# Fixed ScalarE steps of three and of two score tiles in turn, in an attention and FFN kernel

## The chip, the cores and the metric

One core of one Trainium2 chip. The metric is device time in microseconds (us) of one execution. The kernel before takes 705.39 us (median of 3 runs, 705.05 to 706.08). A run counts as slow when it is over 1.5% above the fastest of the same kernel; slow runs are left out of all ratios. Within 2% of before is called the same. The *granted clock* is the share of its full clock that the profile shows for PE. The engines are PE (TensorE), ACT (ScalarE), DVE (VectorE), POOL (GpSimd) and SP (SyncE, which here issues DMAs).

## The reference

A layer norm feeds two branches whose results are added to the input: attention with 32 query heads on one key and value head, and an FFN with a squared ReLU.

```python
xn = _layernorm(x)                      # S = 2048, D = 640
q  = (xn @ wq)  -> 32 heads of 20       # k = xn @ wk, v = xn @ wv: one head of 20
p  = softmax(q k^T * 20 ** -0.5)        # 32 x 2048 x 2048
a  = (p v, heads joined) @ wo
h  = relu(xn @ w1 + b1) ** 2            # F = 1536
return x + a + (h @ w2 + b2)
```

The 32 x 2048 x 2048 scores are made in 32 blocks of 4 heads and 512 queries. Each has 16 key tiles, so there are 32 x 16 x 4 = 2048 score tiles of 128 keys by 512 queries. A tile fills one PSUM bank.

## The kernel before

The program is made by a list scheduler in Python: it keeps a model of each engine's time and appends whichever operation can start first. The order is fixed when the kernel is built. What matters for this change:

- A *step* is one ScalarE instruction that takes the exponential of two or three neighbouring banks. One *score pass* of PE fills them, with up to four tiles side by side in four row groups.
- VectorE takes a part of the tiles away from ScalarE (L1083: one tile from its bank into an integer approximation, then three passes for each set of four tiles on VectorE or GpSimd). Such a tile usually rides along in the row groups that a step's pass leaves free. A pass for a VectorE tile alone is called an *own pass* here; it carries one tile.
- The projections and FFN units, one at a time, also need a bank until VectorE evicts it, and P times V (the exponentials times the values) collects in a bank of its own over a whole block of 4 heads and 512 queries.

```python
NB = 7                      # banks 0 to 6 are shared out freely
PVB = 7                     # bank of P times V
STATIC = False
R3 = 2                      # a step of three only if 3 + R3 banks are free
KEEP = 1                    # one free bank is always left
...
def make_step():
    j = len(steps)
    if par("STATIC"):
        banks = list(SIDES[j % 2])
        if any(bank_state(bk) is None for bk in banks):
            return None
        return build_step(j, banks, 0.0)
    ...
    if len(ok) >= 3 + par("R3"):
        ...                                       # three neighbouring banks
...
def pool_banks():           # banks for VectorE tiles and for units
    if par("STATIC"):
        return [bk for bk in POOLED if bk not in HELD and bank_state(bk) is not None]
    fb = [bk for bk in POOLED if bank_state(bk) is not None]
    return fb if len(fb) > par("KEEP") else []
...
# an own pass: only if the next step's pass is more than DGAP = 0.5 us off,
# and ranked (DQP = 3) behind P times V (1) and the units (0.9, 2)
if rd is not None and (nq is None or nq > max(free["PE"], rd) + par("DGAP")):
    consider("PE", par("DQP"), r[0], ("dqk",) + r[1:])
...
# PE would be idle for long: filler matmuls with zero weights are put in
f_ = Op("fill", "PE", 0.2205, fill_parts())
```

The RULES table sets such knobs by stages of 10 us of ScalarE's time. It had been searched for this kernel.

The softmax here doesn't subtract the row's maximum and nothing guards it: scores larger than these inputs give would overflow.

Of the kernel before, what the change touches and what calls it, by code (L numbers as in the profile page):

```python
# [16 lines left out]
NBLK = QC * G  # L17
# [8 lines left out]
EPS = 1e-5  # L26
# [9 lines left out]
def _pl(z):  # L36
# [9 lines left out]
NB = 7  # L46
PVB = 7
SHARED = (4, 5, 6)
STATIC = False
SIDES = ((0, 1), (2, 3))  # L50
POOLED = tuple(range(NB))
HELD = sum(SIDES, ())
EVP = 0.8
# [27 lines left out]
RULES = {3: {'PVA': 2.1, 'PVD': 2.1, 'R3': 1, 'PP': 0.9},  # L81
         4: {'PVA': 2.1, 'PVD': 2.1, 'R3': 1, 'PP': 0.9, 'WARM': 0.78},
         5: {'D1P': 1, 'MPRIO': 0.5, 'PBIAS': 2.5},
         6: {'D1P': 1, 'MPRIO': 0.5, 'PBIAS': 2.5, 'ND': 1, 'QKP': 0},
         7: {'DQP': 2.05, 'URG': 2, 'PVD': 2.1, 'BEHIND': -0.3},
         8: {'WARM': 0.85, 'DQP': 0.95},
         10: {'ND': 1, 'NOPEN': 3},
         11: {'ND': 1, 'NOPEN': 3},
         12: {'EPS': 0.12},
         13: {'EPS': 0.06, 'EVP': 0.3},  # L90
         15: {'PBIAS': 0},
         17: {'EPS': 0.06},
         18: {'EPS': 0.12},
         19: {'WARM': 0.78, 'PBIAS': 2.5, 'IDLE': 0.3},
         21: {'PBIAS': 0, 'KEEP': 0},
         23: {'EPS': 0.12},
         25: {'R3': 1, 'EVP': 0.3},
         26: {'R3': 1, 'EVP': 0.3, 'IDLE': 0.3, 'PVD': 2.1},
         28: {'EPS': 0.12, 'URG': 3},
         29: {'EPS': 0.12, 'URG': 3, 'KEEP': 3, 'EVP': 1.1, 'ND': 3},  # L100
         31: {'PBIAS': 1, 'D1P': 1, 'PVD': 1.05},
         32: {'PBIAS': 1, 'D1P': 1, 'PVD': 1.05, 'DGAP': 0.8, 'DQP': 0.95, 'SQP': 2, 'R3': 1},
         36: {'PP': 0.9, 'BEHIND': -0.1, 'EVP': 0.3, 'PBIAS': 1.5},
         37: {'URG': 3, 'JIT': 1.0, 'PVD': 1},
         38: {'SQP': 0.7, 'URG': 3},
         39: {'PP': 2.5},
         40: {'PBIAS': 1},
         41: {'PBIAS': 1, 'DGAP': 1.5, 'SQP': 0.7},
         42: {'PBIAS': 1, 'DGAP': 1.5, 'SQP': 2, 'NOPEN': 3, 'ND': 2, 'PVD': 1},
         43: {'PBIAS': 1, 'DGAP': 1.5, 'SQP': 2, 'NOPEN': 3, 'ND': 2, 'PVD': 1, 'R3': 9},  # L110
         44: {'WARM': 0.78, 'KEEP': 3, 'DLAST': 7.5},
         45: {'DGAP': 0.8, 'KEEP': 1, 'D1P': 3},
         48: {'PBIAS': 1},
         49: {'PBIAS': 1, 'R3': 1},
         50: {'PBIAS': 1, 'R3': 1},
         53: {'DLAST': 3.5},
         54: {'DLAST': 3.5, 'EPS': 0, 'EVP': 0.3},
         55: {'DLAST': 3.5, 'EPS': 0, 'EVP': 0.3, 'ND': 1},
         56: {'EVP': 2, 'MPRIO': 1.0},
         57: {'R3': 1, 'ND': 1},  # L120
         58: {'BEHIND': -0.1, 'EPS': 0, 'PP': 4, 'R3': 1},
         59: {'BEHIND': -0.1, 'EPS': 0, 'PP': 4, 'R3': 1, 'DRATE': 0.95, 'DLAST': 10, 'PVA': 2.1},
         60: {'EVP': 1.1},
         61: {'EVP': 1.1, 'SQP': 0.7},
         62: {'EVP': 1.1, 'SQP': 0.7, 'KEEP': 3, 'R3': 1, 'NOPEN': 2, 'D1P': 3},
         64: {'PP': 0.9, 'DRATE': 0.8},
         65: {'R3': 1},
         66: {'R3': 1},
         67: {'EPS': 0.12, 'PVA': 1.05},
         68: {'R3': 0},  # L130
         69: {'R3': 0, 'JIT': 1.1}}
HOOK = None
PRIO = {'NM15': 2.12, 'NM10': 2.88, 'PW2': 0.96}
NBEF = {'AG4': 10.21, 'NM7': 11.5, 'Qe0_1': 10.11, 'PW12': 25.33}
XACT = (1, 3)
QEACT = (0, 1, 2, 3)
# [7 lines left out]
FFN0 = 0.3  # L144
# [4 lines left out]
ACTST = (2, 5, 6)  # L149
POOLXN = (2, 7, 9, 10, 11, 13, 14, 15)  # L150
# [9 lines left out]
                EPS=0.03, JIT=JIT, R3=R3, STATIC=STATIC, PVA=1, PVD=1, D1P=1, PP=4, SQP=2, DQP=3, QKP=0, ND=2, WARM=WARM, KEEP=KEEP)  # L160
# [64 lines left out]
def bass_parallel_sum__grouped_kv_mqa__dense_activation_squared_relu__prompt_kernel(nc, A_x, A_wq, A_wk, A_wv, A_wo, B_x, B_w1, B_b1, B_w2, B_b2, out):  # L225
    es = ExitStack()
    with es:  # L227
# [138 lines left out]
        def mm(out_, l, r, start, stop, tp):  # L366
            return lambda e: e.matmul(out_, l, r, start=start, stop=stop, tile_position=tp)  # L367
# [138 lines left out]
        def fill_parts():  # L506
            return [mm(ps[32 * jj:32 * jj + 32, PVB, :], zeros32[:, :], kT[:, 0:512], False, False, (0, 32 * jj)) for jj in range(4)]

        def warm_parts():
            return [lambda e: e.matmul(ps[:, PVB, :], ones_bf[:, :], hT_tmp[:, 0, :], start=True, stop=True)]  # L510

# [337 lines left out]
# [6 lines that stand above are left out]
                    return None  # L855
                return build_step(j, banks, 0.0)
            t0 = max(free["PE"], horizon() - par("JIT"))
            st_of = {bk: bank_state(bk) for bk in range(NB)}
            ok = [bk for bk in range(NB) if st_of[bk] is not None and st_of[bk] <= t0 + 0.02]
            banks = None  # L860
            if len(ok) >= 3 + par("R3"):
                ap = [(a, a + d, a + 2 * d) for d in (1,) for a in range(NB - 2 * d) if {a, a + d, a + 2 * d} <= set(ok)]
                if ap:
                    banks = list(ap[0])
            if banks is None:
                can = sorted((max(st_of[bk], st_of[bk + 1], t0), bk) for bk in range(NB - 1) if st_of[bk] is not None and st_of[bk + 1] is not None)
                if not can:
                    return None
                banks = [can[0][1], can[0][1] + 1]
            return build_step(j, banks, t0)  # L870
# [50 lines left out]

        def make_pv(b, kt):
            first, last = b not in pv_begun, pv_count[b] == KT - 1
            parts, deps = [], []
            for h in range(HPG):
                o, sl = tile_act[(b, kt, h)]
                deps.append(o)
                parts.append(mm(ps[32 * h:32 * h + 32, PVB, :], vx[:, kt, :], PT[:, sl, :], first, last, (0, 32 * h)))
            deps.append(v_op[kt // 4])
            if first and b > 0:  # L930
                deps.append(tn_op[b - 1])
            return Op(f"PV{b}_{kt}", "PE", 0.222, parts, deps)

        def make_dpv(s, term):
            b, kt, n = s["b"], s["kt"], s["n"]
            first, last = b not in pv_begun, pv_count[b] == KT - 1 and len(s["terms"]) == 1
            src, wgt = tbuf(s["buf"][term]), (vx if term == 0 else vxs[:, term - 1, :, :])
            deps = list(s["made"][term])
            parts = []
            for h in range(HPG):  # L940
                i = s["order"].index(h)
                parts.append(mm(ps[32 * h:32 * h + 32, PVB, :], wgt[:, kt, :], src[:, i * 512:(i + 1) * 512], first, last, (0, 32 * h)))
            deps.append(v_op[kt // 4])
            if term:
                deps.append(vs_op[kt // 4][term - 1])
            if first and b > 0:
                deps.append(tn_op[b - 1])
            return Op(f"DPV{b}_{kt}_{term}", "PE", 0.2205, parts, deps)
# [14 lines left out]
        def emit_norm(b, lastpv):  # L963
            marg = DMARG if b < NBLK - 3 else DMEND
            qc, g = divmod(b, G)
            a = b % NOR
            if b >= NBLK - 2:
                Tn, T2 = OR[:, a, :], QCr[:, 0, :]
                tn = op(f"TN{b}", "DVE", 0.63, lambda e: e.transpose(out=Tn, in_=ps[:, PVB, :]), [lastpv] + or_users[a], prio=0)
# [8 lines left out]
            tn = op(f"TN{b}", "DVE", 0.60, lambda e: e.tensor_copy(out=OR[:, a, :], in_=ps[:, PVB, :]), [lastpv] + or_users[a], prio=0)  # L978
# [62 lines left out]
        def pool_banks():  # L1041

            if par("STATIC"):
                return [bk for bk in POOLED if bk not in HELD and bank_state(bk) is not None]
            fb = [bk for bk in POOLED if bank_state(bk) is not None]
            return fb if len(fb) > par("KEEP") else []
# [5 lines left out]
        def make_dqk(heads):  # L1052
            opn = [s for s in sets[-NL:] if s["left"]]
            fb = pool_banks()
            if not fb or (len(fb) == 1 and behind()):
                return None
# [60 lines left out]
        def tail_bank():  # L1117
            done = not peek_tiles(1)[0]
            bs = [bk for bk in range(NB) if (bk not in HELD or done) and bank_state(bk) is not None]
            if tn_op.get(NBLK - 1) is not None and tn_op[NBLK - 1].fin is not None and not bank_busy[PVB]:  # L1120
                bank_rel[PVB] = bank_rel[PVB] or tn_op[NBLK - 1]
                bs.append(PVB)
            return min(bs, key=lambda bk: (bank_state(bk), bk)) if bs else None
# [68 lines left out]
        while True:  # L1192
# [37 lines left out]
            if b < NBLK and (b == 0 or b - 1 in tn_op):  # L1230
# [76 lines left out]
            elif kind == "qk":  # L1307
                take_step(ap[1])
                heads = [t[2] for t in ap[1]["tiles"]]
                while len(heads) < HPG:  # L1310
# [13 lines left out]
            elif kind == "pv":  # L1324
                pv_begun.add(ap[1])
                pv_of[(ap[1], pv_ready[ap[1]].pop(ap[2])[1])] = o
                finish_pv(ap[1], o)
            elif kind == "dpv":
                pv_begun.add(ap[1])
# [129 lines left out]
```

## Time and profile before

| | before |
|---|---|
| time, us | 705.39 |
| busy: PE, ACT, DVE, POOL | 99%, 98%, 92%, 61% |
| ScalarE steps of two, of three | 665, 50 |
| tiles on ScalarE, on VectorE | 1480, 568 |
| filler groups of four matmuls | 3 |

The chain of work that ended last lies on ScalarE for 95%. From the waits of before (engine, line, what it waited for: us in total, times, longest):

```profile
DVE tmore L1083 <- PE ps L367: 28.2, 83, 1.3
```

VectorE, before one of its score tiles, was idle for 28 us in total until PE had filled the bank.

### The profile page before, as it was taken

To read this page: it belongs to the slowest core of one execution; us is meant where nothing else is said; L and a number is where in the kernel's file an instruction comes from. 1 tells how busy PE (TensorE), PEld (TensorE's weight loads), DVE (VectorE), ACT (ScalarE), POOL (GpSimd) and SP (SyncE) were. 2 spreads that over 40 slices of the span, in tenths; PEclk is the share of its full clock that TensorE was granted. 3 is DMA by queue.
4 is the path that set the end of the run, shared out by engine and by line. 5 is a ranking of instruction groups with operands and counts; after the bars stand their busy time and mean duration, and the time that the engine had idled before them with its cause. 6 is when DMAs were issued, how large, how long until landed. Compare 5 with 4: busy or idle time off the path is not lost.

```text
span 703.6 us, 22608 instructions
## 1 busy us (share of the span) xinstructions
PE 695.0 (99%) x9780; PEld 216.0 (31%) x9781; DVE 645.9 (92%) x1125; ACT 687.5 (98%) x739; POOL 427.3 (61%) x268
## 2 busy tenths in 40 slices
PE   8999999999999999999999999999999999999997
PEld 4422223233322223332322222323333222233333
DVE  7789999999999998989998998899899999999894
ACT  6899999999999999999999999999999999999995
POOL 4767556567566764666568765766665675644253
PEclk9999999999999999999999999999999999999999
DMA  6325422233337701211101001111112100031201
GB/s 201 98 70 153 115 78 58 81 97 80 84 85 160 162 20 25 55 40 37 52 18 40 23 22 28 29 47 26 46 42 51 36 22 23 20 106 51 55 26 39
DMA packets 42016, 44.00 MB, mean 63 GB/s; under 512 B 15540, under 2 KB 32772, under 8 KB 41788
## 3 DMA queue, kind: packets, MB, share of 16 engines
q1 hardware_dynamic: 39132, 36.93, 19.2%
q0 software_dynamic: 2208, 5.25, 3.9%
q8 instruction: 76, 1.25, 0.7%
q10 hardware_dynamic: 576, 0.38, 0.2%
q14 instruction: 24, 0.20, 0.1%
HBM read 28.03 MB, written 14.91 MB: 61 GB/s over the span
## 4 chain that ended last, share of the span: by engine, by line
ACT 95%; PE 4%; DMA 1%; DVE 0%; SPq 0%; issue 0%; DVEq 0%
ACT PT L910 94%; PE ps L367 3%; DMA x_sb<-in_A_x_dram 1%; PE ps L540 1%; ACT xnT L477 0%; ACT OC L421 0%; DVE out_sb L1164 0%; PE ps L568 0%; SPq L384 0%; ACT OC L422 0%; SPq L391 0%; PE ps L510 0%; PE ps L496 0%; DVEq L227 0%; DVE PT L1164 0%
## 5 line engine op out<-in xcount | busy, mean ns | idle before, releaser
L910 ACT ACTIVATE PT<-ps 128x1024 bf16<-128x1024 f32 (+1 forms) x715 | 677.1, 1219 | 3.8 <-PE ps L367 3.8
L1083 DVE TENSOR_SCALAR tmore<-ps 128x512 uint16<-128x512 f32 x568 | 367.4, 683 | 31.7 <-PE ps L367 28.2
L1101 POOL TENSOR_SCALAR tmore<-tmore 128x2048 uint16<-128x2048 uint16 x109 | 206.4, 1900 | 171.1 <-PE ps L367 62.3
L367 PE MATMUL ps<-qT,kT 20*128 20x512 bf16 x2048 | 281.7, 384 | 1.9 <-ACT PT L910 0.8
L1101 POOL TENSOR_SCALAR x_sb<-tmore 128x2048 uint16<-128x2048 uint16 x100 | 189.3, 1902 | 79.4 <-DVE x_sb L1101 24.2
L367 PEld LDWEIGHTS ps<-qT,kT 20*128 20x128 bf16 x2048 | 71.6, 91 | 280.4 <-ACT PT L910 233.1
L367 PE MATMUL ps<-PT,vx 128*32 128x512 bf16 x1480 | 136.9, 386 | 0.2 <-ACT PT L910 0.2
L1101 DVE TENSOR_SCALAR x_sb<-tmore 128x2048 uint16<-128x2048 uint16 x135 | 96.1, 745 | 0.1
L367 PE MATMUL ps<-x_sb,vxs 128*32 128x512 bf16 x940 | 83.2, 382 | 0.0
L367 PE MATMUL ps<-xnT,w_sb 128*32 128x512 bf16 x960 | 77.2, 384 | 0.1
L367 PE MATMUL ps<-w_sb,big 128*32 128x320 bf16 x1536 | 74.5, 302 | 0.0
L367 PE MATMUL ps<-tmore,vxs 128*32 128x512 bf16 x764 | 69.6, 382 | 0.0
L1101 DVE TENSOR_SCALAR tmore<-tmore 128x2048 uint16<-128x2048 uint16 x82 | 61.5, 770 | 0.1
L367 PE MATMUL ps<-tmore,vx 128*32 128x512 bf16 x568 | 55.7, 382 | 0.0
L367 PEld LDWEIGHTS ps<-PT,vx 128*32 128x32 bf16 x1480 | 34.9, 94 | 62.1 <-issue 53.6
L367 PEld LDWEIGHTS ps<-w_sb,big 128*32 128x32 bf16 x1536 | 32.1, 95 | 29.3 <-issue 22.2
L648 DVE TENSOR_SCALAR hT_tmp<-ps,b1col 128x512 bf16<-128x512 f32 x48 | 35.8, 746 | 3.4 <-PE ps L367 2.7
L367 PE MATMUL ps<-xnT,wq_sb 128*32 128x512 bf16 (+1 forms) x480 | 33.7, 356 | 0.2 <-DVE tmore L1083 0.2
L367 PE MATMUL ps<-wo_c,OC 128*32 128x320 bf16 x608 | 30.9, 301 | 0.0
L367 PEld LDWEIGHTS ps<-x_sb,vxs 128*32 128x32 bf16 x940 | 21.3, 95 | 19.9 <-issue 13.4
L367 PEld LDWEIGHTS ps<-xnT,w_sb 128*32 128x32 bf16 x960 | 17.6, 94 | 26.7 <-issue 22.4
L367 PEld LDWEIGHTS ps<-tmore,vxs 128*32 128x32 bf16 x764 | 18.1, 95 | 16.4 <-issue 11.5
(81 smaller groups left out, 259.4 us busy)
## 6 DMA issues: line engine op xcount, KB each, us to landing
xbd<-b2d SPq DMA_DIRECT2D x16, 320.0 KB, 4.4
xbd<-in_A_x_dram POOLq DMA_DIRECT2D x8, 640.0 KB, 5.8
xr<-xbd SPq DMA_DIRECT2D x32, 160.0 KB, 2.4
w_sb<-in_B_w_dram SPq DMA_DIRECT2D x8, 480.0 KB, 4.4
big<-OR SPq DMA_DIRECT2D x71, 40.0 KB
big<-drs SPq DMA_DIRECT2D x71, 40.0 KB
out_dram<-out_sb SPq DMA_DIRECT2D x15, 160.0 KB, 1.8
qT<-QCr SPq DMA_DIRECT2D x108, 20.0 KB
```

The lines of the kernel that those rows point to most:

```text
L367: return lambda e: e.matmul(out_, l, r, start=start, stop=stop, tile_position=tp)
L540: return [(lambda e, dt=dt: e.transpose(out=psbf(bk)[:, dt * 128:(dt + 1) * 128], in_=xn_sb[:, st, dt:D:DT], identity=ident[:])) for dt in ...
L648: o = Op(f"RL{qc}_{f}", "DVE", 0.66, [lambda e: e.tensor_scalar(out=hT_tmp[:, k % 2, :], in0=ps[:, bk, :], scalar1=b1col[:, f:f + 1], scal ...
L910: return Op(f"ACT{st_['j']}", "ACT", 0.05 + 0.4267 * n, [lambda e: e.activation(out=PT[:, s0:s0 + n, :], in_=ps[:, b0:b0 + (n - 1) * db + ...
L1083: d1 = op(f"D1_{n}_{i}", "DVE", 0.60, lambda e: e.tensor_scalar(out=L[:, cs].bitcast(U16), in0=ps[:, bank, :], scalar1=XA, scalar2=XB, op0 ...
L1101: p = op(f"P{j}_{n}", eng, 0.60 if eng == "DVE" else 1.86, lambda e, T=T, j=j, two=two: e.tensor_scalar(out=T.bitcast(U16), in0=L.bitcast( ...
```

## The change

The intent: one ScalarE instruction has a fixed cost, so fewer and larger steps are cheaper. Steps of three and of two alternate on two fixed sets of banks, 0 to 2 and 3 to 4. P times V may move among the three banks left. The table of rules, tuned for the old structure, is emptied, and the start is re-tuned.

```diff
-NB = 7
-PVB = 7
+NB = 8
+PV0 = 7
 SHARED = (4, 5, 6)
-STATIC = False
-SIDES = ((0, 1), (2, 3))
+STATIC = True
+SIDES = ((0, 1, 2), (3, 4))
...
-RULES = {3: {'PVA': 2.1, 'PVD': 2.1, 'R3': 1, 'PP': 0.9},
-   ... (51 stages in all)
+RULES = {}
-PRIO = {'NM15': 2.12, 'NM10': 2.88, 'PW2': 0.96}
-NBEF = {'AG4': 10.21, 'NM7': 11.5, 'Qe0_1': 10.11, 'PW12': 25.33}
+PRIO = {'XN1': 0.13}
+NBEF = {'S4a': 6.0, 'AG5': 10.23, 'PW1': 4.94}
...  (QEACT, FFN0, ACTST, POOLXN: the start)
+        def bank_for(b):
+            if b in pv_bank:
+                return pv_bank[b]
+            can = [(bank_state(bk), -bk) for bk in range(NB) if bank_state(bk) is not None and not (par("STATIC") and bk in HELD)]
+            return -min(can)[1] if can else None
...
-parts.append(mm(ps[32 * h:32 * h + 32, PVB, :], vx[:, kt, :], PT[:, sl, :], first, last, (0, 32 * h)))
+parts.append(mm(ps[32 * h:32 * h + 32, bank, :], vx[:, kt, :], PT[:, sl, :], first, last, (0, 32 * h)))
```

The rest of the diff keeps a bank back for the P times V of the next block, or is knobs that are off here (DJIT, DV) or that work only with free banks.

More of the change, by code (lines that the diff above doesn't have):

```diff
@@ L80 @@
 KEEP = 1
-RULES = {3: {'PVA': 2.1, 'PVD': 2.1, 'R3': 1, 'PP': 0.9},
-         4: {'PVA': 2.1, 'PVD': 2.1, 'R3': 1, 'PP': 0.9, 'WARM': 0.78},
-         5: {'D1P': 1, 'MPRIO': 0.5, 'PBIAS': 2.5},
-         6: {'D1P': 1, 'MPRIO': 0.5, 'PBIAS': 2.5, 'ND': 1, 'QKP': 0},
-         7: {'DQP': 2.05, 'URG': 2, 'PVD': 2.1, 'BEHIND': -0.3},
-         8: {'WARM': 0.85, 'DQP': 0.95},
-         10: {'ND': 1, 'NOPEN': 3},
-         11: {'ND': 1, 'NOPEN': 3},
-         12: {'EPS': 0.12},
-         13: {'EPS': 0.06, 'EVP': 0.3},
-         15: {'PBIAS': 0},
-         17: {'EPS': 0.06},
-         18: {'EPS': 0.12},
-         19: {'WARM': 0.78, 'PBIAS': 2.5, 'IDLE': 0.3},
-         21: {'PBIAS': 0, 'KEEP': 0},
-         23: {'EPS': 0.12},
-         25: {'R3': 1, 'EVP': 0.3},
-         26: {'R3': 1, 'EVP': 0.3, 'IDLE': 0.3, 'PVD': 2.1},
-         28: {'EPS': 0.12, 'URG': 3},
-         29: {'EPS': 0.12, 'URG': 3, 'KEEP': 3, 'EVP': 1.1, 'ND': 3},
-         31: {'PBIAS': 1, 'D1P': 1, 'PVD': 1.05},
-         32: {'PBIAS': 1, 'D1P': 1, 'PVD': 1.05, 'DGAP': 0.8, 'DQP': 0.95, 'SQP': 2, 'R3': 1},
-         36: {'PP': 0.9, 'BEHIND': -0.1, 'EVP': 0.3, 'PBIAS': 1.5},
-         37: {'URG': 3, 'JIT': 1.0, 'PVD': 1},
-         38: {'SQP': 0.7, 'URG': 3},
-         39: {'PP': 2.5},
-         40: {'PBIAS': 1},
-         41: {'PBIAS': 1, 'DGAP': 1.5, 'SQP': 0.7},
-         42: {'PBIAS': 1, 'DGAP': 1.5, 'SQP': 2, 'NOPEN': 3, 'ND': 2, 'PVD': 1},
-         43: {'PBIAS': 1, 'DGAP': 1.5, 'SQP': 2, 'NOPEN': 3, 'ND': 2, 'PVD': 1, 'R3': 9},
-         44: {'WARM': 0.78, 'KEEP': 3, 'DLAST': 7.5},
-         45: {'DGAP': 0.8, 'KEEP': 1, 'D1P': 3},
-         48: {'PBIAS': 1},
-         49: {'PBIAS': 1, 'R3': 1},
-         50: {'PBIAS': 1, 'R3': 1},
-         53: {'DLAST': 3.5},
-         54: {'DLAST': 3.5, 'EPS': 0, 'EVP': 0.3},
-         55: {'DLAST': 3.5, 'EPS': 0, 'EVP': 0.3, 'ND': 1},
-         56: {'EVP': 2, 'MPRIO': 1.0},
-         57: {'R3': 1, 'ND': 1},
-         58: {'BEHIND': -0.1, 'EPS': 0, 'PP': 4, 'R3': 1},
-         59: {'BEHIND': -0.1, 'EPS': 0, 'PP': 4, 'R3': 1, 'DRATE': 0.95, 'DLAST': 10, 'PVA': 2.1},
-         60: {'EVP': 1.1},
-         61: {'EVP': 1.1, 'SQP': 0.7},
-         62: {'EVP': 1.1, 'SQP': 0.7, 'KEEP': 3, 'R3': 1, 'NOPEN': 2, 'D1P': 3},
-         64: {'PP': 0.9, 'DRATE': 0.8},
-         65: {'R3': 1},
-         66: {'R3': 1},
-         67: {'EPS': 0.12, 'PVA': 1.05},
-         68: {'R3': 0},
-         69: {'R3': 0, 'JIT': 1.1}}
@@ L132 @@
+DJIT = 9.0
+DV = 9
+D1P = 1
+RULES = {}
 HOOK = None
-PRIO = {'NM15': 2.12, 'NM10': 2.88, 'PW2': 0.96}
-NBEF = {'AG4': 10.21, 'NM7': 11.5, 'Qe0_1': 10.11, 'PW12': 25.33}
+PRIO = {'XN1': 0.13}
+NBEF = {'S4a': 6.0, 'AG5': 10.23, 'PW1': 4.94}
 XACT = (1, 3)
-QEACT = (0, 1, 2, 3)
+QEACT = (0, 1)
 STOP = None
@@ L143 @@
 EARLYK = "F"
-FFN0 = 0.3
+FFN0 = 0.6
 OUT0 = 0.5
@@ L148 @@
 QCPOS = 0
-ACTST = (2, 5, 6)
-POOLXN = (2, 7, 9, 10, 11, 13, 14, 15)
+ACTST = (0, 2, 4)
+POOLXN = (7, 9, 10, 11, 13, 14, 15)
 ROWP = (-0.5, 0.6, 0.8, 1.2)
@@ L159 @@
 DEFAULTS = dict(EVP=EVP, PBIAS=PBIAS, MPRIO=MPRIO, DGAP=DGAP, DLAST=DLAST, DRATE=DRATE, BEHIND=BEHIND, IDLE=IDLE, URG=URG, NOPEN=NOPEN,
-                EPS=0.03, JIT=JIT, R3=R3, STATIC=STATIC, PVA=1, PVD=1, D1P=1, PP=4, SQP=2, DQP=3, QKP=0, ND=2, WARM=WARM, KEEP=KEEP)
+                EPS=0.03, JIT=JIT, R3=R3, STATIC=STATIC, PVA=1, PVD=1, D1P=D1P, PP=4, SQP=2, DQP=3, QKP=0, ND=2, WARM=WARM, KEEP=KEEP, DJIT=DJIT, DV=DV)
 class Ctr:
@@ L506, in fill_parts @@
         def fill_parts():
-            return [mm(ps[32 * jj:32 * jj + 32, PVB, :], zeros32[:, :], kT[:, 0:512], False, False, (0, 32 * jj)) for jj in range(4)]
+            return [mm(ps[32 * jj:32 * jj + 32, pv_bank[pv_blk[0]], :], zeros32[:, :], kT[:, 0:512], False, False, (0, 32 * jj)) for jj in range(4)]
         def warm_parts():
-            return [lambda e: e.matmul(ps[:, PVB, :], ones_bf[:, :], hT_tmp[:, 0, :], start=True, stop=True)]
+            return [lambda e: e.matmul(ps[:, PV0, :], ones_bf[:, :], hT_tmp[:, 0, :], start=True, stop=True)]
         def need_te(sts):
@@ L857, in make_step @@
             t0 = max(free["PE"], horizon() - par("JIT"))
-            st_of = {bk: bank_state(bk) for bk in range(NB)}
+            keep = kept()
+            st_of = {bk: bank_state(bk) if bk != keep else None for bk in range(NB)}
             ok = [bk for bk in range(NB) if st_of[bk] is not None and st_of[bk] <= t0 + 0.02]
@@ L920, in after_act, with kept, pv_begin @@
                     pv_ready[key[0]].append(("A", key[1]))
+        pv_bank = {0: PV0}
+        bank_busy[PV0] = True
+        def bank_for(b):
[3 more added lines that the diff above has]
+            return -min(can)[1] if can else None
+        def kept():
+            b = pv_blk[0]
+            return bank_for(b) if b < NBLK and b not in pv_begun else None
+        def pv_begin(b):
+            if b not in pv_begun:
+                pv_bank[b] = bank_for(b)
+                bank_busy[pv_bank[b]] = True
+                pv_begun.add(b)
         def make_pv(b, kt):
@@ L924, in make_pv @@
             parts, deps = [], []
+            bank = bank_for(b)
             for h in range(HPG):
@@ L927, in make_pv @@
                 deps.append(o)
-                parts.append(mm(ps[32 * h:32 * h + 32, PVB, :], vx[:, kt, :], PT[:, sl, :], first, last, (0, 32 * h)))
+                parts.append(mm(ps[32 * h:32 * h + 32, bank, :], vx[:, kt, :], PT[:, sl, :], first, last, (0, 32 * h)))
             deps.append(v_op[kt // 4])
-            if first and b > 0:
-                deps.append(tn_op[b - 1])
+            if first:
+                deps.append(bank_rel[bank])
             return Op(f"PV{b}_{kt}", "PE", 0.222, parts, deps)
@@ L939, in make_dpv @@
             parts = []
+            bank = bank_for(b)
             for h in range(HPG):
                 i = s["order"].index(h)
-                parts.append(mm(ps[32 * h:32 * h + 32, PVB, :], wgt[:, kt, :], src[:, i * 512:(i + 1) * 512], first, last, (0, 32 * h)))
+                parts.append(mm(ps[32 * h:32 * h + 32, bank, :], wgt[:, kt, :], src[:, i * 512:(i + 1) * 512], first, last, (0, 32 * h)))
             deps.append(v_op[kt // 4])
@@ L945, in make_dpv @@
                 deps.append(vs_op[kt // 4][term - 1])
-            if first and b > 0:
-                deps.append(tn_op[b - 1])
+            if first:
+                deps.append(bank_rel[bank])
             return Op(f"DPV{b}_{kt}_{term}", "PE", 0.2205, parts, deps)
@@ L966, in emit_norm @@
             a = b % NOR
+            pb = pv_bank[b]
             if b >= NBLK - 2:
                 Tn, T2 = OR[:, a, :], QCr[:, 0, :]
-                tn = op(f"TN{b}", "DVE", 0.63, lambda e: e.transpose(out=Tn, in_=ps[:, PVB, :]), [lastpv] + or_users[a], prio=0)
+                tn = op(f"TN{b}", "DVE", 0.63, lambda e: e.transpose(out=Tn, in_=ps[:, pb, :]), [lastpv] + or_users[a], prio=0)
+                tn.frees = pb
                 rc = op(f"RC{b}", "DVE", 0.155, lambda e: e.reciprocal(out=Tn[:, DH:512:32], in_=Tn[:, DH:512:32]), [tn], prio=0)
@@ L977, in emit_norm @@
                 return
-            tn = op(f"TN{b}", "DVE", 0.60, lambda e: e.tensor_copy(out=OR[:, a, :], in_=ps[:, PVB, :]), [lastpv] + or_users[a], prio=0)
+            tn = op(f"TN{b}", "DVE", 0.60, lambda e: e.tensor_copy(out=OR[:, a, :], in_=ps[:, pb, :]), [lastpv] + or_users[a], prio=0)
+            tn.frees = pb
             tn_op[b] = tn
@@ L1041, in pool_banks @@
         def pool_banks():
+            keep = kept()
             if par("STATIC"):
-                return [bk for bk in POOLED if bk not in HELD and bank_state(bk) is not None]
-            fb = [bk for bk in POOLED if bank_state(bk) is not None]
+                return [bk for bk in POOLED if bk not in HELD and bk != keep and bank_state(bk) is not None]
+            fb = [bk for bk in POOLED if bk != keep and bank_state(bk) is not None]
             return fb if len(fb) > par("KEEP") else []
@@ L1055, in make_dqk @@
             if not fb or (len(fb) == 1 and behind()):
+                return None
+            if max(free["DVE"], free["PE"]) + sum(o.dur for o in dve_q if o.frees is not None) > free["PE"] + 0.43 + par("DJIT"):
                 return None
@@ L1119, in tail_bank @@
             bs = [bk for bk in range(NB) if (bk not in HELD or done) and bank_state(bk) is not None]
-            if tn_op.get(NBLK - 1) is not None and tn_op[NBLK - 1].fin is not None and not bank_busy[PVB]:
-                bank_rel[PVB] = bank_rel[PVB] or tn_op[NBLK - 1]
-                bs.append(PVB)
             return min(bs, key=lambda bk: (bank_state(bk), bk)) if bs else None
@@ L1229, in bass_parallel_sum__grouped_kv_mqa__dense_activation_squared_relu__prompt_kernel @@
             b = pv_blk[0]
-            if b < NBLK and (b == 0 or b - 1 in tn_op):
+            if b < NBLK and (b == 0 or b - 1 in tn_op) and bank_for(b) is not None:
                 for k, (kind, x) in enumerate(pv_ready[b]):
@@ L1309, in bass_parallel_sum__grouped_kv_mqa__dense_activation_squared_relu__prompt_kernel @@
                 heads = [t[2] for t in ap[1]["tiles"]]
+                if len(heads) == 2 and not par("STATIC") and sum(1 for bk in POOLED if bank_state(bk) is not None and bank_state(bk) <= o.start + 0.06) >= par("DV"):
+                    can = [bk for bk in range(NB - 1) if all(k != kept() and bank_state(k) is not None and bank_state(k) <= o.start + 0.06 for k in (bk, bk + 1))]
+                    st_ = build_step(len(steps), [can[0], can[0] + 1], 0.0) if can else None
+                    if st_ is not None and len(st_["tiles"]) == 2 and not set(t[2] for t in st_["tiles"]) & set(heads):
+                        rd = st_["qk"].ready()
+                        if rd is not None and rd <= o.start + 0.06:
+                            st_["qk"].dur = 0.005
+                            commit(st_["qk"])
+                            st_["qk"].lat = 0.425
+                            take_step(st_)
+                            heads += [t[2] for t in st_["tiles"]]
                 while len(heads) < HPG:
@@ L1324, in bass_parallel_sum__grouped_kv_mqa__dense_activation_squared_relu__prompt_kernel @@
             elif kind == "pv":
-                pv_begun.add(ap[1])
+                pv_begin(ap[1])
                 pv_of[(ap[1], pv_ready[ap[1]].pop(ap[2])[1])] = o
@@ L1328, in bass_parallel_sum__grouped_kv_mqa__dense_activation_squared_relu__prompt_kernel @@
             elif kind == "dpv":
-                pv_begun.add(ap[1])
+                pv_begin(ap[1])
                 s_, term = ap[3], ap[4]
```

## The prediction

> **What bounds the kernel now.** I read the page's busy shares and its chain first, then ScalarE's timeline, its instructions by form, a ten-microsecond timeline in the middle, and the waits. Busy shares and the chain:
>
> ```profile
> PE 695.0 (99%) x9780; PEld 216.0 (31%) x9781; DVE 645.9 (92%) x1125; ACT 687.5 (98%) x739; POOL 427.3 (61%) x268
> ACT 95%; PE 4%; DMA 1%; DVE 0%; SPq 0%; issue 0%; DVEq 0%
> ```
>
> The chain is ScalarE for 95% of the span. ScalarE's own timeline, and the by-form list of its instructions:
>
> ```profile
> 15.30 12.46 ACT L910 ACTIVATE PT<-ps 128x1024 bf16<-128x1024 f32 x13 [1.05 <-PE ps L367]
> 28.15 1.94 ACT L910 ACTIVATE PT<-ps 128x1024 bf16<-128x1024 f32 x2 [0.39 <-PE ps L367]
> 32.44 662.70 ACT L910 ACTIVATE PT<-ps 128x1536 bf16<-128x1536 f32 x700 [2.35 <-PE ps L367]
> ...
> L910 ACT ACTIVATE PT<-ps 128x1024 bf16<-128x1024 f32 x665 | 621.9, 1190 | 1.4 <-PE ps L367 1.4
> L910 ACT ACTIVATE PT<-ps 128x1536 bf16<-128x1536 f32 x50 | 79.0, 1609 | 2.3 <-PE ps L367 2.3
> ```
>
> From 32.44 us on, 700 exponentials run without a visible gap until 695.14. There are 665 x 2 + 50 x 3 = 1480 ScalarE tiles of 128x512; the other 568 of the 2048 score tiles go to VectorE (568 evictions at L1083, then three passes for each set of four). So the time is: start (32.44, with 15 steps = 30 tiles done), 1450 tiles on ScalarE, and 703.6 - 695.1 = 8.5 us of tail. What matters is how many tiles ScalarE gets, and what a tile costs there.
>
> PE is no idle partner, as a stretch of the timeline shows:
>
> ```profile
> 400.93 0.62 PE L367 MATMUL ps<-xnT,w_sb 128*32 128x512 bf16 x8
> 401.52 0.10 PEld L367 LDWEIGHTS ps<-qT,kT 20*128 20x128 bf16 x3 [0.47 <-ACT PT L910]
> 401.52 0.39 PE L367 MATMUL ps<-qT,kT 20*128 20x512 bf16 x3
> ...
> 401.84 0.34 PEld L367 LDWEIGHTS ps<-xnT,w_sb 128*32 128x32 bf16 x12 [0.23 <-issue]
> 401.84 0.83 PE L367 MATMUL ps<-xnT,w_sb 128*32 128x512 bf16 x12
> 401.99 0.69 DVE L1083 TENSOR_SCALAR tmore<-ps 128x512 uint16<-128x512 f32 x1
> ...
> 402.60 0.10 PEld L367 LDWEIGHTS ps<-qT,kT 20*128 20x128 bf16 x3 [0.42 <-ACT PT L910]
> ...
> 402.73 0.75 DVE L648 TENSOR_SCALAR hT_tmp<-ps,b1col 128x512 bf16<-128x512 f32 x1
> ```
>
> A score pass (here two ScalarE tiles and one VectorE tile) starts at 401.52 and the next work at 401.84: 0.32. The three groups of four that follow take 3 x 0.22 = 0.66 of the 0.76 to the next pass: 0.10 more. A score pass thus takes 0.42 of PE, however many of its four row groups it uses; a group of four 512-wide matmuls takes 0.22, and one of four 320-wide ones 0.137 (four of them between 301.99 and 302.64, less that 0.10). Count from the page: 3752 + 1420 matmuls 512 wide are 1293 groups, 284 us; 2208 of 320 are 552 groups, 76 us; over 700 passes at 0.42 are 300 us. The sum, 660, is the 662 us of ScalarE's unbroken run. PE is full too, and VectorE is 92 to 97% busy in most of the 100 us windows. This is a balance of three engines.
>
> **What the Trainium skill says.** "ScalarE: Activation LUTs", section on what ACT_TABLE_LOAD costs, gives 0.833 ns per element and a fixed part per ACTIVATE that partly overlaps the next. The trace agrees: the two forms differ by 1609 - 1190 = 419 ns for 512 elements (0.82 ns each). With 0.4267 us a tile, 1450 tiles are 618.7 of the 662.7 us; less 0.29 by which the last instruction's 1.19 exceeds its share, 43.7 us remain for 700 instructions, 62 ns each. "TensorEngine Tiling (Array Packing)", Key Properties, says that changing the tiling mode drains TensorE; the 0.23 "issue" idle after each score pass agrees. "SBUF — State Buffer", Who interferes with whom, says a two-port VectorE operation and a GpSimd one exclude each other. The trace fits this: 427 us of POOL and 158 us of VectorE passes make 585 of some 660 even without the two-input multiplies. "Perfetto Trace Analysis", Identifying the Most-Contended Engine, warns that consistent bubbles can mean too few buffers. Before has none on ScalarE, whose banks are found freely among seven.
>
> **The change part by part.**
> 1. Steps of three and two in turn. Five tiles cost 5 x 0.4267 + 2 x 0.062 = 2.257 us, 0.4515 each. Before costs 662.4 / 1450 = 0.4568. With the same 1480 tiles the gain is 1450 x 0.0053 = 7.7 us, all of it on the path: 592 instructions instead of 715. Time 705.4 - 7.7 = 697.7.
> 2. Fewer score passes. If each step still has one pass, 592 instead of 715 is 123 x 0.42 = 52 us of PE freed. It lies beside ScalarE and gives no time by itself; it makes room for extra passes.
> 3. Fixed sets. The three-bank set must refill during one two-tile step. A three-tile step lasts 1.61 from its start, and the two-tile step behind it ends its share 2.26 after that same start. So 0.65 is left for wake-up, the 0.39 matmul and wake-up, about 0.5 in all (the VectorE eviction above starts 0.47 after its pass, so a wake-up is some 0.08). About 0.15 is free; a PE group of 0.22 in the way can sometimes cost some tens of ns. The two-bank set has about 0.43 more. I allow 1 us in total.
> 4. The banks left. Three of eight remain, one of which collects PV. So two serve VectorE tiles and all projections and FFN units. Before had seven for everything but PV: two steps in flight held four, about three were left, and one had to stay free. A VectorE tile holds its bank from 401.52 to 402.68 above, some 1.25 with the wake-up. FFN1's unit (from 400.93, its eviction ending at 403.48) holds one 2.6; an output unit near 300 us (first matmul 300.15, eviction ending 305.09) 4.9. With my estimates of 3.2 for 48 FFN1 units, 3.8 for 8 partial ones, 5 for 24 outputs and 3 for 18 projections, that is some 360 bank-us over 655 us: 0.55 bank on average. So 1.45 banks are left for VectorE tiles.
>  In the new rhythm score passes come 0.92 and 1.34 us apart by turns. A tile put in at a pass is too late for the one 0.92 later (1.25), so a bank takes one riding tile per 2.26 us: 1.45 tiles per five on ScalarE. Before's steady mix is 568 of about 1998 tiles (without the first 30 and the last 20), 1.99 per five. The lack of 0.5 must come from extra passes in the long gap. The freed 52 us of PE hold about 120 of those, 0.4 per cycle. I take 1.9: 1.9 / 6.9 x 1998 = 550 VectorE tiles, 18 fewer, and 1498 on ScalarE. Cost 18 x 0.4515 = 8.1 us.
> 5. The tuned table of per-stage rules goes, and the priorities of the start change. These set only order. I give them no amount of their own, but they widen the range; the start, with many transposes and projections in two banks, could lose or win some 3 us.
>
> Sum: 705.4 - 7.7 + 1.0 + 8.1 = 706.8. I shade this by 1 us, since the start and the late-stage tuning of the new version seem to have been redone for it: 706.
>
> **The rivals.** (a) Banks are the tighter limit: extra passes often come too late, the mix falls to 1.6 per five, so 1.6 / 6.6 x 1998 = 484 tiles on VectorE, 84 fewer: 38 us, about 736. For it: hold times and only two banks. Against it: VectorE and PE both get room, evictions start at once, units finish sooner. (b) Freed PE is used: the 28.2 us that VectorE now waits for PE at L1083 (83 times) turn into more sets. A set costs VectorE about 2.6 + 1.5 x 0.75 = 3.7 us, so at most 7 sets, 28 tiles, 12.6 us, about 686. Against it: the shared port has little left for more passes. (c) ScalarE waits at each three-bank refill, 0.1 us x 300 = 30 us, about 728 with the mix of before. Against it: the 0.15 spare. (d) The mix stays and only instructions are saved: 698.
>
> **Range and chances.** 706 lies between (a) and (d); one VectorE tile per five more or less is worth far more than every fixed cost. A mix of 2.05 to 1.72 per five gives 581 to 511 tiles, thus 693 to 725 by the same sum; I take 692 to 723. Faster by over 2% (under 691.3) needs rival (b): 0.10. Slower by over 2% (over 719.5) needs a mix under about 1.77 or rival (c): 0.20. Within: 0.70.
>
> **What would show it.** Right: about 600 exponentials, half of each form, unbroken; per five tiles 2.26 us; VectorE evictions 530 to 570; some 100 score passes more than ScalarE steps; VectorE idle some per cent higher, mostly waiting for PE at L1083; PE waiting longer for ScalarE. Wrong: ScalarE idle of over 5 us in total behind PE (rival c); evictions under 510 (a) or over 580 (b); the unbroken run beginning after 36 us; the fixed cost per instruction no longer 62 ns.

Three corrections to its text. Its sentence on consistent bubbles stands in "Perfetto Trace Analysis" in the section Optimization Strategy, which follows the one it names. It calls the fixed cost of 62 ns a step's own, though it is an average; the shortest and most frequent distance from the start of a step of two to the next in the trace is 904 ns, and from one of three 1330 ns. They differ by 426 ns for one tile, so some 51 ns are fixed and about 11 more are small waits. And its sum of 585 us is compatible with VectorE and GpSimd excluding each other, but does not show it.

## The result

The changed kernel takes 753.14 us (753.05 to 753.17, 3 runs). The ratio to before is 1.0675 (95% interval 1.0651 to 1.0699): 6.75% slower. Ratios here are the mean time of one kernel's fast runs over that of the other's fast runs of the same rounds, so they are not quite the ratio of the quoted medians.

Busy shares and the chain of the changed kernel, the answer to the first lines in the prediction:

```profile
PE 716.6 (95%) x10359; PEld 241.2 (32%) x10361; DVE 580.0 (77%) x990; ACT 733.5 (98%) x662; POOL 292.0 (39%) x195
ACT 94%; PE 4%; DMA 1%; DVE 1%; SPq 0%; issue 0%; DVEq 0%
```

ScalarE is as busy as before and still carries the chain. VectorE fell from 92% to 77% and GpSimd from 61% to 39%. Its work is what has moved. ScalarE's timeline and the groups by form (the exponential, now L864; then VectorE's score tiles, now L1066):

```profile
14.72 6.88 ACT L864 ACTIVATE PT<-ps 128x1536 bf16<-128x1536 f32 x6 [1.98 <-PE ps L320]
24.30 6.88 ACT L864 ACTIVATE PT<-ps 128x1536 bf16<-128x1536 f32 x6 [2.69 <-PE ps L320]
31.43 8.37 ACT L864 ACTIVATE PT<-ps 128x1536 bf16<-128x1536 f32 x7 [0.24 <-PE ps L320]
41.23 701.65 ACT L864 ACTIVATE PT<-ps 128x1024 bf16<-128x1024 f32 x621 [1.43 <-PE ps L320]
...
L864 ACT ACTIVATE PT<-ps 128x1536 bf16<-128x1536 f32 x320 | 522.6, 1633 | 4.9 <-PE ps L320 4.9
L864 ACT ACTIVATE PT<-ps 128x1024 bf16<-128x1024 f32 x320 | 388.6, 1214 | 1.4 <-PE ps L320 1.4
```
```profile
L1066 DVE TENSOR_SCALAR tmore<-ps 128x512 uint16<-128x512 f32 x448 | 299.5, 686 | 112.3 <-PE ps L320 109.7
```

From 41.23 us on, 621 steps run without a gap. The steps number 640 instead of 715, but they hold 320 x 3 + 320 x 2 = 1600 tiles and not 1480. VectorE evicts 448 tiles and not 568, and it waits 109.7 us for PE before them, four times as long as before (28.2).

The 47.8 us between the two spans (751.4 and 703.6) can be split into parts. The costs per tile come from the same spans, so the sum must close; what it tells is the size of each part. The first 19 steps of the changed kernel are 48 tiles and end at 41.23; before had 30 tiles at 32.44 and would have 48 at 32.44 + 18 x 0.457 = 40.66, so the start costs 0.6. After that the changed kernel has 1552 tiles; 701.65 - 0.29 over 1552 is 0.4519 us each. Before had 1432 tiles at 0.4568. The cheaper steps save 1432 x 0.0049 = 7.0, and 120 more tiles cost 120 x 0.4519 = 54.2. Together 0.6 - 7.0 + 54.2 = 47.8. The tails are both 8.5. So the change does what it was meant to do per tile, and the loss is that VectorE gets 120 tiles fewer.

A stretch in the middle shows how this comes about (start, duration, engine, line, operation, count, and in brackets the idle time before):

```profile
404.10 0.10 PEld L320 LDWEIGHTS ps<-qT,kT 20*128 20x128 bf16 x3 [0.42 <-ACT PT L864]
...
404.43 1.05 PE L320 MATMUL ps<-kT,zeros 128*32 128x512 bf16 x16
405.21 0.68 DVE L1084 TENSOR_SCALAR tmore<-tmore 128x2048 uint16<-128x2048 uint16 x1
405.40 0.10 PEld L320 LDWEIGHTS ps<-qT,kT 20*128 20x128 bf16 x3 [0.42 <-ACT PT L864]
...
407.54 0.39 PE L320 MATMUL ps<-qT,kT 20*128 20x512 bf16 x3 [0.54 <-ACT PT L864]
```

Between two passes PE computes sixteen filler matmuls: the scheduler has nothing else for it. The page lists them:

```profile
L320 PE MATMUL ps<-kT,zeros 128*32 128x512 bf16 x936 | 74.9, 381 | 0.0
```

These are 234 groups of four; at 0.22 us each that is 51 us of PE. So PE had room, and nothing used it. That a PE row is 95% busy does not show this; the group's operands do.

### The profile page after: what moved, and what is told of

The parts are those of the page before. It is cut to its first block, busy times and chain, and to the rows that moved or that the text cites. A ratio compares the mean times of both kernels' runs of the same rounds, so it can differ in the third digit from the quotient of the medians.

```text
span 751.4 us, 23326 instructions
## 1 busy us (share of the span) xinstructions
PE 716.6 (95%) x10359; PEld 241.2 (32%) x10361; DVE 580.0 (77%) x990; ACT 733.5 (98%) x662; POOL 292.0 (39%) x195
## 4 chain that ended last, share of the span: by engine, by line
ACT 94%; PE 4%; DMA 1%; DVE 1%; SPq 0%; issue 0%; DVEq 0%
ACT PT L864 94%; PE ps L320 3%; DMA x_sb<-in_A_x_dram 1%; PE ps L463 0%; PE ps L493 0%; DVE out_sb L1144 0%; PE ps L521 0%; PE ps L449 0%; ACT OC L374 0%; SPq L337 0%; DVE OR L379 0%; DVE kT L507 0%; PE ps L428 0%; SPq L344 0%; ACT xnT L430 0%
## 5 line engine op out<-in xcount | busy, mean ns | idle before, releaser
L864 ACT ACTIVATE PT<-ps 128x1536 bf16<-128x1536 f32 (+1 forms) x640 | 723.8, 1424 | 6.4 <-PE ps L320 6.3
L1066 DVE TENSOR_SCALAR tmore<-ps 128x512 uint16<-128x512 f32 x448 | 299.5, 686 | 112.3 <-PE ps L320 109.7
L320 PE MATMUL ps<-qT,kT 20*128 20x512 bf16 x2048 | 267.9, 384 | 27.7 <-ACT PT L864 24.8
L1084 POOL TENSOR_SCALAR tmore<-tmore 128x2048 uint16<-128x2048 uint16 x81 | 153.4, 1898 | 242.4 <-DVE x_sb L1084 85.8
L1084 POOL TENSOR_SCALAR x_sb<-tmore 128x2048 uint16<-128x2048 uint16 x56 | 106.4, 1902 | 169.6 <-DVE x_sb L1084 114.5
L320 PE MATMUL ps<-PT,vx 128*32 128x512 bf16 x1600 | 152.9, 387 | 0.6 <-DVE OR L957 0.5
L320 PE MATMUL ps<-kT,zeros 128*32 128x512 bf16 x936 | 74.9, 381 | 0.0
L320 PE MATMUL ps<-x_sb,vxs 128*32 128x512 bf16 x740 | 65.9, 382 | 0.2
L320 PE MATMUL ps<-tmore,vxs 128*32 128x512 bf16 x604 | 52.3, 381 | 0.0
L320 PEld LDWEIGHTS ps<-kT,zeros 128*32 128x32 bf16 x936 | 21.7, 95 | 21.7 <-issue 12.6
```

What stands on the lines that cost most here:

```text
L320: return lambda e: e.matmul(out_, l, r, start=start, stop=stop, tile_position=tp)
L864: return Op(f"ACT{st_['j']}", "ACT", 0.05 + 0.4267 * n, [lambda e: e.activation(out=PT[:, s0:s0 + n, :], in_=ps[:, b0:b0 + (n - 1) * db + ...
L1066: d1 = op(f"D1_{n}_{i}", "DVE", 0.60, lambda e: e.tensor_scalar(out=L[:, cs].bitcast(U16), in0=ps[:, bank, :], scalar1=XA, scalar2=XB, op0 ...
L1084: p = op(f"P{j}_{n}", eng, 0.60 if eng == "DVE" else 1.86, lambda e, T=T, j=j, two=two: e.tensor_scalar(out=T.bitcast(U16), in0=L.bitcast( ...
```

## The experiments

Theories at stake. *Banks*: the third bank of the three-bank set was one that VectorE tiles had lived on. *Order*: the emptied rules and the new start cost the time. *Refill*: fixed sets make ScalarE wait. *Rhythm*: the unequal distances of score passes (0.92 and 1.34 us) lose tiles. *Own passes*: PE had room for passes of VectorE tiles alone, but they were ranked last. The tile counts in the expectations could be given beforehand, since the order is fixed in the built program.

### The kernel before without its rules

```diff
-RULES = {3: {...}, ...}
+RULES = {}
```

> The kernel before with its table of per-stage rules emptied, nothing else. As built it gives 560 tiles to VectorE and 1488 to ScalarE (568 and 1480 before). Bank theory (the lost time came from the bank that VectorE's tiles lost): the rules are a small part, 710 to 716 us, and evictions stay near 560. Order theory (the emptied rules and the changed start cost the 48 us): 735 us or more, with ScalarE idle between its steps. Extra-pass theory says nothing of this one.

Measured: 715.86 us median (5 runs, four of them 715.1 to 716.2, one 722.25 at a granted clock of 0.988), ratio 1.0145 (1.0129 to 1.0162). The rules are worth some 10 us (without them VectorE has 8 tiles fewer), at the upper end of what the bank theory allowed, and far from 48.

### The changed kernel with free banks

```diff
-STATIC = True
+STATIC = False
```

> The changed kernel with fixed sets off: banks found freely, eight in the pool, the start, the movable PV bank and the empty rules all as in the changed kernel. As built: 556 VectorE tiles, 719 steps of two and 18 of three. Bank theory: 712 to 724 us, so nearly all of the 48 us is gone. Order theory: it stays within 10 us of the changed kernel, 743 us or more. Refill theory (fixed sets make ScalarE wait): also 712 to 724, so this run does not tell it from the bank theory; the next two do.

Measured: 721.46 us, ratio 1.0233 (1.0213 to 1.0253), with 556 VectorE tiles. All the rest of the change (start, movable PV bank, empty rules) is in this kernel, and it is 16 us slower than before, not 48. Order as the main cause falls.

### Fixed sets of two and two

```diff
-SIDES = ((0, 1, 2), (3, 4))
+SIDES = ((0, 1), (2, 3))
```

> The changed kernel with fixed sets of two and two banks in place of three and two: fixed sets stay, one more bank is left for the rest. As built: 552 VectorE tiles, 748 steps of two. Bank theory: 712 to 724 us, about as with free banks. Refill theory: fixed sets still cost most of the loss, 735 us or more. Order theory: 743 us or more.

Measured: 721.82 us, ratio 1.0231 (1.0216 to 1.0246). Its ScalarE timeline has 724 steps in one unbroken run:

```profile
41.34 664.02 ACT L864 ACTIVATE PT<-ps 128x1024 bf16<-128x1024 f32 x724 [2.82 <-PE ps L320]
```

VectorE has 552 tiles:

```profile
L1066 DVE TENSOR_SCALAR tmore<-ps 128x512 uint16<-128x512 f32 x552 | 359.3, 684 | 38.4 <-PE ps L320 35.7
```

Fixing the sets costs next to nothing against free banks: 0.4 us. This is a net figure. ScalarE's waits for PE before its steps are 6.1 us here and 14.9 with free banks (in a profile at a clock of 0.995), and the tail is 15.0 us long and not 8.5. The refill theory falls.

### Fixed sets of two and two, with the freed bank withheld

```diff
-SIDES = ((0, 1, 2), (3, 4))
-HELD = sum(SIDES, ())
+SIDES = ((0, 1), (2, 3))
+HELD = sum(SIDES, ()) + (4,)
```

> As the run before, fixed sets of two and two, but the freed bank is withheld from everything, so that PV, VectorE tiles and units have three banks, as in the changed kernel. As built: 452 VectorE tiles (448 in the changed kernel), 798 steps of two. Bank theory: the tiles fall by some 100 for this one bank and the time is 755 to 768 us, 4 to 12 us slower than the changed kernel, since five tiles in steps of two cost 2.29 and not 2.26 us. Rhythm theory (unequal gaps of 0.92 and 1.34 us between score passes are what loses the tiles, each bank catching one pass per 2.26 and not per 1.83 us): about 515 tiles and 725 to 735 us.

Measured: 762.55 and 762.47 us in the two fast runs (two more were slow, 776 and 787 at clocks of 0.98 and 0.965, and are left out); ratio 1.0808 (1.0786 to 1.0829). Its steps in the long run, and its row for VectorE's score tiles:

```profile
42.26 709.73 ACT L864 ACTIVATE PT<-ps 128x1024 bf16<-128x1024 f32 x774 [3.01 <-PE ps L320]
...
L1066 DVE TENSOR_SCALAR tmore<-ps 128x512 uint16<-128x512 f32 x452 | 306.6, 687 | 126.6 <-PE ps L320 124.5
```

Only one bank differs from the kernel before this one, and between the start and the tail it stays empty: 552 tiles become 452, VectorE's wait for PE before them rises from 35.7 to 124.5 us, and the time rises by 40.7 us. The 50 more steps alone are 50 x 0.917 = 45.9 us; some 6.5 come back at the end, where the kernel with the bank has a tail of 15.0 us and this one 8.5.

Against the changed kernel, which leaves the same three banks, this one is 9.4 us slower at almost the same tiles (452 and 448). That is the gain of steps of three: 158 steps fewer at 62 ns are 9.8 (four VectorE tiles fewer take back 1.8 of it, and a long run that begins 1.0 us earlier, at 41.23 and not 42.26, adds to it). The rhythm theory falls with it: passes at equal distances of 0.92 us did not catch more tiles. So does a rival that I had not named: a pass for three ScalarE tiles leaves one row group for a riding tile, and one for two leaves two. Here every pass leaves two, and VectorE gets no more.

### The changed kernel with own passes ranked up

```diff
-DGAP = 0.5
+DGAP = 0.3
-DQP=3
+DQP=0.95
```

> The changed kernel with score passes for VectorE tiles alone ranked above PV work, and allowed when the next step's pass is 0.3 us away and not 0.5. As built: 242 such passes and not 55, 500 VectorE tiles and not 448, 58 filler groups and not 267. Extra-pass theory (PE had room, but these passes were ranked last): about half of the 48 us returns, 728 to 742 us, ScalarE still unbroken in the main. If instead the extra passes only delay PV and the refills, ScalarE waits appear and the time stays above 748 us.

Measured: 739.99 us (737.76 to 744.75), ratio 1.0494 (1.0445 to 1.0542). There are 52 more VectorE tiles and 13 us less time, inside the range that I had given, but a quarter of the loss and not half. Fifty-two tiles at 0.4519 are 23.5 us. ScalarE's waits for PE (11.5 us where the changed kernel has 6.3) and a tail that is 14.1 and not 8.5 us long took back some 11 (the profile's run was granted 0.991 of the clock):

```profile
ACT PT L864 <- PE ps L320: 11.5, 10, 2.7
```

### The changed kernel without own passes

```diff
-DGAP = 0.5
+DGAP = 99.0
```

> The changed kernel with no score pass for VectorE tiles alone: all of them ride on ScalarE's passes. As built: 432 VectorE tiles. If riding is the limit that the prediction worked out (1.45 tiles per five, 434 tiles) the mix is 432 to 1616 and the time 757 to 763 us; that would say that the changed kernel's own passes gained it only 16 tiles. If the own passes matter more than that: under 415 tiles and over 770 us.

Measured: 760.34 us (760.18 to 760.81), ratio 1.0779 (1.0761 to 1.0797). Riding alone brings 432 tiles. The changed kernel's 55 own passes net it 16 tiles and 7.2 us (16 x 0.4519 = 7.2), and the 242 of the run before net 68. An own pass is thus worth 0.28 to 0.29 of a tile: with 55 of them 448 - 55 = 393 tiles ride, with 242 only 258, and without any 432. Mostly an own pass takes the place of a riding tile. That it does so by taking the bank is argued, not shown by itself.

### The kernel before with one bank less

```diff
-RULES = {3: {...}, ...}
+RULES = {}
-NB = 7
+NB = 6
```

> The kernel before with empty rules and one bank fewer in its pool (six and not seven), steps still of two wherever banks are found, no fixed sets, PV in its own bank. As built: 476 VectorE tiles and 1572 on ScalarE (560 and 1488 with seven). Bank theory: some 37 us slower than the kernel with empty rules, 745 to 757 us, all of it ScalarE tiles. Every other theory (fixed sets, unequal steps, order, start): no part of the change is here, so about 714 us.

Measured: 755.91, 751.47 and 750.63 us in the fast runs (a slow one of 772.25 is left out), ratio 1.0668 (1.0632 to 1.0705). The profile is of the slow run, so I take only its counts: 476 evictions instead of 560. Nothing of the changed structure is in this kernel. Against the kernel without its rules (715.86) the one bank costs 35.6 us and 84 tiles, and the two together are as slow as the change.

### The kernel before, taking three banks whenever it can

```diff
-RULES = {3: {...}, ...}
+RULES = {}
-R3 = 2
+R3 = 0
```

> The kernel before with empty rules, which takes a step of three whenever three neighbouring banks are free (before: only when five are). Banks are not fixed. As built: 291 steps of three and 355 of two, 464 VectorE tiles. Bank theory: larger steps take the banks that VectorE's tiles would have had, so 745 to 762 us although nothing is fixed. Theory of fixed sets: without fixing, steps of three only save instructions, so 705 to 714 us.

Measured: 765.21 us (756.86 to 765.59), ratio 1.0818 (1.0762 to 1.0873).

```profile
L1033 DVE TENSOR_SCALAR tmore<-ps 128x512 uint16<-128x512 f32 x464 | 304.7, 685 | 98.3 <-PE ps L317 96.6
ACT PT L860 <- PE ps L317: 20.2, 22, 3.9
```

With 291 steps of three on free banks VectorE falls to 464 tiles. That the larger steps themselves take the banks is the reading that the expectation made beforehand. The median is 3 us above what I expected. Three of the four runs were granted 0.985 to 0.989 of the clock; the one at 0.998 took 756.86, inside the range. The profile, in which ScalarE waits 20 us for PE (22 waits), is of a run at 0.988, so how much of this wait is due to the order is open.

### The changed kernel with its order searched

Eleven global knobs, the two of the own passes among them:

```diff
-EVP = 0.8, DRATE = 0.95, URG = 4.0, PBIAS = 0.6, DGAP = 0.5, D1P = 1, IDLE = 0.3
+EVP = 2, DRATE = 0.8, URG = 4, PBIAS = 2.5, DGAP = 0.3, D1P = 0.1, IDLE = 0.1
-PP=4, DQP=3, ND=2
+PP=2.5, DQP=0.95, ND=3
```

(URG and the eleventh, DLAST, kept their values.)

> The changed kernel with its fixed sets of three and two and the best of a search over its global ordering settings (eleven of them, own passes ranked above PV among them). As built: 504 VectorE tiles, 309 steps of three, 308 of two, 228 own passes. If the structure is the limit: 730 to 740 us, better than the run with own passes alone by little, and still over 3% behind before. If the emptied rules were the cause of most of the loss: a search over the order should bring it to 720 us or less.

Measured: 746.62 us (745.35 to 750.3), ratio 1.0584 (1.0554 to 1.0614): a miss. It has four tiles more on VectorE than the kernel with own passes alone and is 6.6 us slower. Its windows (length; busy us and count of PE, PEld, DVE, ACT, POOL; granted clock; DMA) show where:

```profile
100.00:200.00 100.00, 98.81 (x1265) 30.77 (x1265) 75.61 (x122) 93.08 (x82) 59.95 (x32) 0.90 0.27 73
200.00:300.00 100.00, 94.89 (x1209) 27.80 (x1205) 74.69 (x123) 92.18 (x82) 59.71 (x36) 0.93 0.38 86
300.00:400.00 100.00, 99.44 (x1366) 32.84 (x1365) 80.35 (x124) 100.00 (x90) 73.94 (x40) 1.00 0.15 38
```

In two stretches PE was granted 0.90 and 0.93 of its clock, and just there ScalarE was busy only 92 to 93%. All four runs have a mean clock of 0.97 to 0.976. That the lower clock is what makes ScalarE wait is only argued from this coincidence. It fits that one and the same kernel takes longer in runs with a lower clock: the one with own passes ranked up 737.76 at 0.995 and 744.75 at 0.986, the one without rules 715.08 at 1.0 and 722.25 at 0.988. So the times of these kernels hold a part that is not their order's. No order that I found brings this structure near 720 us. Even without a wait after the start, the 1544 ScalarE tiles of this one would take some 727 us (estimate: the changed kernel's 41.2 for the first 48, 1496 x 0.4519, its tail of 8.5, and 1.7 between span and time).

### The changed kernel again

> The changed kernel once more, unaltered, so that it stands beside the tuned one on one chip: 752 to 755 us, 448 VectorE tiles.

Measured: 753.21 us (753.13 to 753.59), ratio 1.0671 (1.0653 to 1.0689), on the same chip as the tuned one.

### The ladder

Each kernel is one rung from the next (medians; of the withheld bank the mean of the fast runs):

| kernel | us | step | VectorE tiles |
|---|---|---|---|
| before | 705.4 | | 568 |
| without rules | 715.9 | +10.5 | 560 |
| start, movable PV bank, eighth bank in the pool | 721.5 | +5.6 | 556 |
| fixed sets of two and two | 721.8 | +0.4 | 552 |
| one bank withheld | 762.5 | +40.7 | 452 |
| that bank joined to a set: three and two | 753.1 | -9.4 | 448 |

No version here beats the kernel before. Steps of three pay 9 us and the bank they stand on costs 41.

## Why the prediction was wrong

It said 706 us (692 to 723) with "same" at 0.7. The measured 753.14 is far outside. By its own steps:

1. *Steps of three and two in turn: 0.4515 us a tile.* Right. Measured 0.4519, and the saving of 7.0 us at equal tiles was predicted as 7.7. The run with the withheld bank shows the same gain by itself, 9.4 us.
2. *Fewer score passes free 52 us of PE.* Wrong, and the 51 us of filler match it by luck. The 52 came from 592 steps. The kernel as built has 640 steps and 55 own passes, 695 passes where before has 717 (715 steps and, as built, 2 own passes), so passes free 22 x 0.42 = 9 us. Ninety groups fewer of P times V (a set of four VectorE tiles takes four, four ScalarE tiles one) free 20 more, and the execution is 47.8 us longer. Of these 77 us, 51 went into filler and 26 are added idle time of PE (span less busy: 8.6 before, 34.8 after). PE's room is thus mostly a result of the loss.
3. *Fixed sets cost about 1 us.* Right: 0.4 us net between free banks and fixed sets of two, and in the changed kernel four ScalarE waits, none of them after 41.23 us.
4. *Banks.* The first half was right in its numbers. Units take 363 bank-us in the trace of the changed kernel (estimate: 360), measured by matching the records in order with the operations of the program, from the first weight load to the end of the eviction. Riding alone was worked out as 1.45 tiles per five. The run without own passes gives 432 tiles to 1616, which is 1.34 per five over the whole run and about 1.4 without the start and the tail. The step that failed is the next sentence, "The lack of 0.5 must come from extra passes in the long gap", with "I take 1.9". PE's room was taken for a supply of tiles. The kernel made 55 own passes, ranked last as the code says, which net 16 tiles. Even 242 passes net only 68, since most take the place of a riding tile. The mix came to 448 / 1600 x 5 = 1.40 per five. In the prediction's own sum, 120 tiles at 0.4515 are 54 us where it put 8.
5. *Rules: no amount of their own.* They are worth 10.5 us on the kernel before. What part of this the changed kernel lost with them stays open, since rules made for free banks do not fit it.

Its rival (a) named the cause, though not its full size: a mix of 1.6 and 736 us. It was set aside because "VectorE and PE both get room, evictions start at once". They did, measured in the same way: the mean hold of a VectorE tile's bank fell from 1.61 to 1.38 us, and the units' from 412 to 363 bank-us in all. But a bank that is free is worth nothing before the next pass. Tiles and units held 617 + 363 = 980 bank-us; two banks over some 700 us are 1400. The rest is time in which a bank stood free; that it was waiting for a pass is argued, not measured. The explanation by rhythm that stood beside it, one riding tile per 2.26 us for a bank, agreed with the count but is not the cause: with passes every 0.92 us the same banks carry 452 tiles. That 1.45 came so near is therefore partly luck.

Of its signs, the unbroken run (but from 41 us, which the prediction called a sign of being wrong; it cost 0.6 us, since 48 tiles and not 30 were done by then), half of each form, 2.26 us per five tiles and VectorE and PE waiting longer all came. The 530 to 570 evictions did not, nor did some 100 passes more than steps (55). ScalarE's 6.3 us behind PE are over the 5 that should have meant rival (c), but all of them lie in the start.

## What to carry to other kernels

When several engines share the PSUM banks, count for each consumer how many banks it can hold at a time and how many tiles a bank turns over, before and after, and trust that count over an engine's spare time: an idle engine makes no supply if the thing that is scarce is a bank. Larger instructions save a fixed cost per instruction (here 9 us) but hold more banks at once, and the bank must come from someone (here 41 us). If an idle engine is to make up for it, first test what one more pass of it brings (here 0.28 of a tile). A saturated engine without gaps can still be slowed by lack of buffers, by being given more of the work: look at the counts per engine and at who waits for whom on the engine that is *not* the bound.

## What the Trainium skill lacked or had wrong

- "Perfetto Trace Analysis", Optimization Strategy, looks for missing buffers as gaps on the engine that should be saturated. Here ScalarE had none (621 steps unbroken); the lack showed as 109.7 us of VectorE waits for PE (28.2 before) and as a shifted share of tiles.
- "PSUM — Partial Sum Buffer" says to evacuate promptly but gives no way to price a bank. Here one bank of eight was 100 score tiles and 40.7 us of some 720.
- "ScalarE: Activation LUTs", What ACT_TABLE_LOAD costs: 186 ns less an overlap of 93 leaves 93 ns fixed for an ACTIVATE with immediate operands. Reading PSUM, the steps here came 904 and 1330 ns apart at best, so 51 ns fixed, as the 51 ns in "Perfetto Trace Analysis", Optimizing Scalar/DVE Operations, says.
- "TensorEngine Tiling (Array Packing)", Key Properties, gives no size for the drain on a change of mode. Here PE's weight loads stood idle 0.23 us after each score pass, and a pass with both its changes took 0.42 us, where four matmuls of the same width took 0.22 between their like: some 0.1 us a change (estimate from these).
